# Attention results stored once a batch in whole rows, and registers of the final branch read ahead of the last product

## The chip, the cores and the metric

The kernel runs on one core of a Trainium2 chip. TensorE (PE) multiplies, VectorE (DVE), ScalarE (ACT) and GpSimd (POOL) work element by element, SyncE (SP) issues transfers, and 16 DMA engines move data between the on-chip memory and DRAM. Each engine has its own instruction stream; semaphores order them. The metric is the time of one execution on the device, in microseconds (us); lower is better.

## The reference

Two blocks one after the other. First an attention that is linear in the sequence (8 batches, 8 heads, 576 tokens, 64 channels a head): softmax of q over the channels, softmax of k over the tokens, then two small products. Its result, with the heads side by side, is x, 576 rows of 512 numbers for each batch. Then a mixture of depths: of each batch's 576 tokens, the 128 with the highest score pass through a two-layer network, and what it gives is added to their rows; all other rows of the output are x itself.

```python
kv = einsum('bhsd,bhse->bhde', softmax(k, tokens), v)
x = einsum('bhsd,bhde->bhse', softmax(q, channels), kv)   # then heads side by side
scores = einsum('bsd,d->bs', x, w_gate)
out = x.copy()
for b in range(B):
    top = argpartition(-scores[b], 128)[:128]
    ye = maximum(x[b, top] @ w1, 0) @ w2                  # 512 -> 1024 -> 512
    out[b, top] = x[b, top] + sigmoid(scores[b, top])[:, None] * ye
```

## The kernel before, in words

**Units.** The attention is cut into 16 units; a unit is one batch and half of its heads (`units`, line 96; `NQ` is 2). Unit 2b is the first half of the heads of the kernel's batch b, unit 2b+1 the second half. `place(b)` (line 93) gives the batch in memory, (b - 1) mod 8, so the kernel's first batch is the last in memory.

**One unit.** `load` fetches k, v and q; `k_exp`, `q_exp` (ACT) take exponentials; `v_copy` lays v beside a column of ones; `kv_mm` forms the product of k and v on PE and `kv_out` scales it on DVE; `q_t` or `q_blocks` turns q; `x_mm` forms the result on PE; `x_sums` takes the score sums; `x_scale` (line 436) divides by the softmax sum and writes the tile `xs[b]`. That tile holds both units of a batch. A partition holds nine tokens in all, split into two groups: partitions 0 to 63 hold the first five token rows of each run of nine, partitions 64 to 127 the other four. So `x_store(u)` (line 449) issues two DMAs a unit from SP: 64 partitions times 5 rows, and 64 partitions times 4 rows, each row 1 KB, half a row of the output.

**One batch.** After both of its units, `score`, `score_row` and `compare` rank the tokens; `hits` marks the chosen ones; `find` (line 514) makes the list of row numbers with a small product on PE; `fetch` (line 530) reads those rows back from the output in DRAM with an indirect DMA of POOL, so it must wait until the stores of that batch have landed. The row range that it names begins at row 0, so it waits for the indirect writes of the batches below it too. `turn` (line 566) transposes the rows on PE, `mlp1` (line 582) and `mlp2` (line 597) are the two layers, `finish` (line 635) adds the result to the rows on DVE, and `put` (line 604) writes them to the output with an indirect DMA. The first batch takes another way (`select`), without reading back.

**Order.** The order of all instructions is written out by hand. Stage s works on unit s of the attention while it loads unit s+3 and runs the network of the batch before. `queues(s, last)` (line 842) sets what SP issues in stage s, from the string `QUEUE` (line 824): `x+0 kv+3 q+3` is the store of unit s, then k and v of unit s+3, then q of unit s+3. In stage 5 the stores of units 0 and 1 (`x-5 x-4`) follow at the end. Stage 3 issues the stores of units 2 and 3 itself. SP takes its queue strictly in order. Some loads wait for a product of the stage (`last`) and for the fourth load before them (`way`).

**The end.** `last_product` (line 619) computes the second layer of the last batch in two halves, 16 products each, and writes each half by an indirect DMA. After it, `nc.values_load` (line 989) reads the number `number` (made by `count_good`, line 738) into a register of every engine. `tc.If` (line 990) then enters `general()`, a slower way for inputs out of range, when not all checks held; with these inputs it is passed by.

Of the kernel before, what the change touches and what calls it, by code (L numbers as in the profile page):

```python
# [17 lines left out]
def kernel(  # L18
# [23 lines left out]
    nc = tc.nc  # L42
    B, H, S, D = q.shape
    DM, F = moe_w1.shape
    P = 128
    R = 5
    N2 = R - 1
    T = R + N2
# [5 lines left out]
    NQ = H // 4  # L54
# [33 lines left out]
    def part(i):  # L88
        return slice(64 * i, 64 * i + 64)
# [3 lines left out]
    def place(b):  # L93
        return (b - 1) % B
# [77 lines left out]
    def clear(u):  # L172
        for what in "kv":
# [5 lines left out]
                                               ap=[[DM, 1], [1, DM]]))  # L179
# [239 lines left out]
    xs = {}  # L419
# [28 lines left out]

    def x_store(u):
        b, qd = units[u]  # L450
        for n, rows in enumerate((R, N2)):
            nc.sync.dma_start(
                out=bass.AP(tensor=out.tensor, offset=out[place(b), n * R].offset + 4 * D * qd,
                            ap=[[T * DM, 64], [DM, rows], [1, 4 * D]]),
                in_=xs[b][part(n), :rows, qd].rearrange("p r i a d -> p r (i a d)"))


    def score(b, up=2):
# [200 lines left out]
    def each(step, b, *args):  # L659
        for n in range(n_sl):  # L660
            step(b, n, *args)
# [26 lines left out]
    def general():  # L688
# [4 lines left out]
        for b in range(B):  # L693
            for u in (NQ * b, NQ * b + 1):
                load(u, "kvq", flat=True)
                shift(u)
                k_exp(u)
                q_exp(u, 0)
                q_exp(u, 1)
                v_copy(u)  # L700
                kv_mm(u)
                kv_out(u)
                q_t(u, 0)
                q_t(u, 1)
                for i in range(2):
                    x_mm(u, i)
                    x_out(u, i)
                x_store(u)
            score(b, 0)
            score_row(b, 1.0)  # L710
            for r in range(R):
                compare_exact(b, r)
            for step in (hits, find, fetch, gate):
                each(step, b)
            each(turn, b)
            for f in range(KF):
                each(mlp1, b, f)
            for f in range(KF):
                each(mlp2, b, f)
            each(finish, b)  # L720
            each(put_done, b)

    CHECKS = 6

    def in_range():

        rq, rk = qrec.rearrange("p u a i n -> p (u a i n)"), krec.rearrange("p u n -> p (u n)")
        sc = s_all.rearrange("p b r -> p (b r)")
        ends = md.tile([P, CHECKS], F32, tag="ends", name="ends", bufs=1)
        good = md.tile([P, CHECKS], BF16, tag="good", name="good", bufs=1)  # L730
        for n, (src, op, bound) in enumerate(((rq, OP.max, 1.0 / LOW), (rk, OP.max, 1.0 / LOW), (sc, OP.max, FAR),
                                              (rq, OP.min, LOW), (rk, OP.min, LOW), (sc, OP.min, -FAR))):
            nc.vector.tensor_reduce(out=ends[:, n:n + 1], in_=src, axis=AX.X, op=op)
            nc.vector.tensor_scalar(good[:, n:n + 1], ends[:, n:n + 1], bound, None,
                                    op0=OP.is_le if op == OP.max else OP.is_ge)
        return good

    def count_good(good):
        g_ps = pair("kv")[:, 0]
        nc.tensor.matmul(out=g_ps[:1, :CHECKS], lhsT=ones_b[:, :1], rhs=good, start=True, stop=True)  # L740
        total = md.tile([1, 1], F32, tag="total", name="total", bufs=1)
        nc.vector.reduce_sum(out=total, in_=g_ps[:1, :CHECKS], axis=AX.X)
        number = md.tile([1, 1], I32, tag="number", name="number", bufs=1)
        nc.vector.tensor_copy(out=number, in_=total)
        return number
# [79 lines left out]
    number = good = None  # L825
    for s in range(LAG, NU + LAG - 1):
# [15 lines left out]
        def queues(s, last):  # L842
            for what in QUEUE.get(s, QUEUE["odd" if s % 2 else "even"]).split():
                name, u = what[:-2], s + int(what[-2:])
                if name == "x":
                    if u < NU:
                        x_store(u)
                elif u < NU:
                    load(u, name, after=last, odd=False if name == "q" and u in SPREAD else None)
                    last = None  # L850
# [14 lines left out]
        if s == LAG:  # L865
# [7 lines left out]
            x_out(2, 0)  # L873
            x_out(2, 1)
            x_store(2)
            load(5, "q")
            pieces(2)
# [32 lines left out]
        else:  # L910
# [59 lines left out]
            if good is not None and number is None:  # L970
                pieces(0, to=6)
                number = count_good(good)
# [11 lines left out]
        if s == NU:  # L984
            good = in_range()

    each(last_product, B - 1)

    ok = nc.values_load(number[0:1, 0:1], min_val=0, max_val=CHECKS * P)
    with tc.If(ok != CHECKS * P):  # L990
        general()

# [23 lines left out]
```

## Time and profile before

| | us |
|---|---|
| median of three runs | 206.79 |
| lowest, highest run | 206.05, 208.31 |
| the profiled execution, its own time | 204.39 |
| span of that execution, first to last instruction | 202.6 |
| PE busy, DVE busy, ACT busy, POOL busy | 190.1, 127.2, 91.7, 39.3 |
| DMA issues of the store (line 452) | 32, median 0.636 each on SP |

The profile is one execution with the hardware profiler on. Times in it count from the start of the span. "Busy" is the time that an engine's own instructions took; reading registers, waiting and issuing transfers are not in it. The 40 slices cut the span into equal parts, each digit a busy share in tenths. The chain is followed back from the last instruction: at each step to what released it. A row `SPq L452 <- DVE xs L439: 13.4, 5, 3.9` says that SP's queue waited at line 452 for the DVE instruction of line 439, for 13.4 us in total, 5 times, at most 3.9.

### The profile page before, as it was taken

The page shows a single profiled execution, that of the slowest core. Times are in us where ns is not written, and L with a number is a line of the kernel's source. Part 1 is how long each engine was busy: PE and PEld are TensorE (multiplying, and loading weights), DVE is VectorE, ACT ScalarE, POOL GpSimd, SP SyncE. Part 2 cuts the span into 40 slices and gives each one's busy share as a digit, 9 for nine tenths or more (in the row PEclk, how much of TensorE's full clock was granted, in tenths as well). Part 3 has the DMA queues.
Part 4 walks back from the last instruction along what each step waited for, and adds up shares of the span by engine and source line. Part 5 has one row for each costly group of instructions (what it writes and reads, how often), then busy time and mean ns, then how long its engine had stood idle before and what let it go on. Part 6 is the DMA issues. An engine that isn't in the chain of part 4 may idle for free.

```text
span 202.6 us, 6720 instructions
## 1 busy us (share of the span) xinstructions
PE 190.1 (94%) x2817; PEld 146.7 (72%) x2817; DVE 127.2 (63%) x395; ACT 91.7 (45%) x136; POOL 39.3 (19%) x107
## 2 busy tenths in 40 slices
PE   7889899989999999999999999999999999999950
PEld 3567789986599657977598749964895789469840
DVE  5778935889278364866678477838697879232000
ACT  3477776590946555629046543654363021111100
POOL 7302100101020400412040402210040122313130
PEclk9999999999999999999999999999999999999997
DMA  6999999999888999999899899999996156211110
GB/s 212 394 293 315 379 368 373 363 383 374 246 263 241 300 348 330 260 283 308 191 280 275 293 236 269 255 323 201 269 279 231 55 120 151 68 54 55 57 40 23
DMA packets 35255, 49.43 MB, mean 244 GB/s; under 512 B 2449, under 2 KB 28049, under 8 KB 35218
## 3 DMA queue, kind: packets, MB, share of 16 engines
q1 hardware_dynamic: 33296, 42.72, 69.5%
q0 software_dynamic: 1776, 5.92, 9.5%
q8 instruction: 24, 0.39, 0.8%
q10 hardware_dynamic: 146, 0.30, 0.5%
q14 instruction: 13, 0.11, 0.2%
HBM read 37.39 MB, written 11.53 MB: 241 GB/s over the span
## 4 chain that ended last, share of the span: by engine, by line
PE 75%; DMA 15%; SPq 4%; ACT 1%; issue 1%; POOL 0%; POOLq 0%; DVE 0%; ACTq 0%
PE mm L591 26%; PE mm L601 24%; DMA k<-in_k_dram 15%; PE kv L336 8%; PE x L414 6%; PE mm L628 3%; PE x L384 2%; PE mm L571 2%; PE kv L479 2%; SPq L152 2%; SPq L187 1%; PE x L405 1%; ACT ke L289 1%; PE mm L520 1%; SPq L146 1%
## 5 line engine op out<-in xcount | busy, mean ns | idle before, releaser
L591 PE MATMUL mm<-xT,w 128*128 128x128 f32 x512 | 61.8, 278 | 0.5 <-DVE xT L579 0.3
L591 PEld LDWEIGHTS mm<-xT,w 128*128 128x128 f32 x512 | 58.7, 192 | 2.3 <-ACT xT L579 1.0
L601 PE MATMUL mm<-w,hT 128*128 128x512 f32 x112 | 52.5, 603 | 0.0
L493 DVE SCALAR_TENSOR_TENSOR junk<-srow,s,not_before 128x576 bf16<-128x576 f32 x40 | 32.7, 818 | 4.4 <-ACT srow L485 3.3
L601 PEld LDWEIGHTS mm<-w,hT 128*128 128x128 f32 x112 | 19.7, 190 | 17.7 <-issue 17.2
L289 ACT ACTIVATE ke<-k 128x1280 f32<-128x1280 f32 (+1 forms) x16 | 20.2, 1261 | 10.2 <-DMA k<-in_k_dram 10.2
L439 DVE TENSOR_TENSOR xs<-x,qrec 128x640 f32<-128x640 f32 (+1 forms) x31 | 23.4, 756 | 0.6 <-issue 0.3
L336 PEld LDWEIGHTS kv<-v_ones,ke 128*64 128x64 f32 x560 | 17.5, 137 | 4.5 <-issue 3.2
L336 PE MATMUL kv<-v_ones,ke 128*64 128x65 f32 x560 | 19.4, 224 | 0.5 <-ACT srow L485 0.5
L414 PE MATMUL x<-kv_w,qT 64*64 64x66 f32 x960 | 19.4, 221 | 0.1
L307 ACT COPY v_ones<-v 128x1280 f32<-128x1280 f32 x14 | 17.6, 1254 | 3.4 <-DMA v<-in_v_dram 3.4
L594 ACT ACTIVATE hT<-mm 128x512 f32<-128x512 f32 x16 | 9.5, 596 | 20.5 <-PE mm L591 20.5
L414 PEld LDWEIGHTS x<-kv_w,qT 64*64 64x64 f32 x960 | 17.1, 134 | 1.8 <-issue 1.2
L463 POOL TENSOR_TENSOR s<-s_all,valid_r 128x5 f32<-128x5 f32 x8 | 1.5, 192 | 85.0 <-DVE s_all L461 85.0
L534 POOL DMA_INDIRECT xr<-out_dram,idx x8 | 8.1, 1012 | 48.8 <-DVE no L526 31.6
L579 ACT COPY xT<-mm 128x512 f32<-128x512 f32 x7 | 4.1, 585 | 27.3 <-PE mm L571 27.3
L391 ACT COPY qT<-x 128x640 f32<-128x640 f32 (+1 forms) x18 | 10.8, 648 | 12.3 <-PE x L384 11.6
L302 ACT ACTIVATE qe<-q 128x640 f32<-128x640 f32 (+1 forms) x22 | 13.9, 677 | 3.5 <-DMA q<-in_q_dram 3.5
L345 DVE RECIPROCAL krec<-kv 128x2 f32<-128x2 f32 x16 | 2.7, 169 | 18.0 <-PE kv L336 17.3
L639 DVE SCALAR_TENSOR_TENSOR o<-mm,g,xr 128x512 f32<-128x512 f32 x6 | 4.5, 751 | 11.4 <-PE mm L601 11.4
L485 ACT ACTIVATE srow<-kv 128x576 f32<-128x576 f32 x7 | 4.5, 648 | 12.3 <-PE kv L479 12.3
L431 DVE RECIPROCAL qrec<-x 128x10 f32<-128x10 f32 (+1 forms) x31 | 6.6, 213 | 4.8 <-PE x L405 4.3
(125 smaller groups left out, 204.2 us busy)
## 6 DMA issues: line engine op xcount, KB each, us to landing
out_dram<-xs SPq DMA_DIRECT2D x16, 320.0 KB, 4.5
k<-in_k_dram SPq DMA_DIRECT2D x14, 320.0 KB, 4.9
v<-in_v_dram SPq DMA_DIRECT2D x14, 320.0 KB, 6.5
w<-in_moe_w_dram SPq DMA_DIRECT2D x8, 512.0 KB, 7.6
out_dram<-xs SPq DMA_DIRECT2D x16, 256.0 KB, 5.5
q<-in_q_dram SPq DMA_DIRECT2D x7, 576.0 KB, 6.7
q<-in_q_dram SPq DMA_DIRECT2D x14, 280.0 KB, 7.0
k<-in_k_dram SPq DMA_DIRECT2D x14, 256.0 KB, 6.6
```

Of the source, the lines that this page charges most:

```text
L289: nc.scalar.activation(out=ke, in_=view(raw["k"][u % LD], u not in FLAT), func=AF.Exp)
L302: nc.scalar.activation(out=st["qe", u][:, r0:r1], in_=qr[:, r0:r1], func=AF.Exp)
L307: engine.copy(out=out_v, in_=in_v)
L336: nc.tensor.matmul(out=kv_ps[part(i), a, :D + 1], lhsT=ke[:, 2 * i + a, r], rhs=vo[:, 2 * i + a, r], start=(r == 0), stop=(r == N2))
L391: nc.scalar.copy(out=to, in_=src)
L414: last = nc.tensor.matmul(out=to, lhsT=rows, rhs=kw[part(i), a], start=True, stop=True)
L439: nc.vector.tensor_mul(xs[b][:, :n, qd, :, a].rearrange("p r i d -> p i r d"), x[:, :, :, :D], qrec[:, u, a, :, :n].to_broadcast([P, 2, n, ...
L493: nc.vector.scalar_tensor_tensor(junk, st["srow", b], st["s", b][:, r:r + 1], not_before[:, r], op0=OP.subtract, op1=OP.is_ge, accum_out=s ...
L534: nc.gpsimd.indirect_dma_start(out=xr[:m], out_offset=None, in_=out_rows[:(place(b) + 1) * S], in_offset=bass.IndirectOffsetOnAxis(ap=st[" ...
L591: st["piece"] = nc.tensor.matmul(out=h_ps[:, f % 4 * m:(f % 4 + 1) * m], lhsT=w1[:, d, f * P:(f + 1) * P], rhs=xT[:, d, :m], start=(d == 0 ...
L594: nc.scalar.activation(out=hT[:, f - 3:f + 1, :m], in_=h_ps[:, :4 * m].rearrange("p (f c) -> p f c", f=4), func=AF.Relu)
L601: st["piece"] = nc.tensor.matmul(out=st["y", b, n][:m], lhsT=st["hT", b, n][:, f, :m], rhs=w2[:, f], start=(f == 0), stop=(f == KF - 1))
```

## The change

Two edits. The store of a batch's first unit is left out. The store of its second unit writes the whole rows of both: 64 partitions, each five rows of 2 KB that lie one after the other in memory and in the tile, 10 KB in one run; and 64 partitions of four rows, 8 KB. The number of bytes is the same. In stage 3, the store of unit 2 falls away and that of unit 3 carries both; in stage 5, `x-5` falls away and `x-4` carries units 0 and 1.

The second edit moves the reading of the registers from behind `last_product` to in front of it.

```diff
     def x_store(u):
         b, qd = units[u]
+        if qd < NQ - 1:
+            return
         for n, rows in enumerate((R, N2)):
             nc.sync.dma_start(
-                out=bass.AP(tensor=out.tensor, offset=out[place(b), n * R].offset + 4 * D * qd,
-                            ap=[[T * DM, 64], [DM, rows], [1, 4 * D]]),
-                in_=xs[b][part(n), :rows, qd].rearrange("p r i a d -> p r (i a d)"))
+                out=bass.AP(tensor=out.tensor, offset=out[place(b), n * R].offset, ap=[[T * DM, 64], [1, rows * DM]]),
+                in_=xs[b][part(n), :rows].rearrange("p r q i a d -> p (r q i a d)"))
...
+    ok = nc.values_load(number[0:1, 0:1], min_val=0, max_val=CHECKS * P)
     each(last_product, B - 1)
 
-    ok = nc.values_load(number[0:1, 0:1], min_val=0, max_val=CHECKS * P)
     with tc.If(ok != CHECKS * P):
         general()
```

## The prediction

> **What bounds the kernel.** I read the page first (busy shares, slices, the chain), then busy time by stretch, then the stores and whoever waits for them, then the end.
>
> ```profile
> span 202.6 us, 6720 instructions
> PE 190.1 (94%) x2817; PEld 146.7 (72%) x2817; DVE 127.2 (63%) x395; ACT 91.7 (45%) x136; POOL 39.3 (19%) x107
> DMA  6999999999888999999899899999996156211110
> PE 75%; DMA 15%; SPq 4%; ACT 1%; issue 1%; POOL 0%; POOLq 0%; DVE 0%; ACTq 0%
> ```
>
> TensorE and the DMA engines are both nearly full, and the chain says who decides when: its 15% of DMA all lies before 40 us (loads of k), where no store has been issued. From there it runs over TensorE. The stretches 42 to 180, 180 to 195.2 and 195.2 to the end confirm it (time, then busy time and count of PE, PEld, DVE, ACT, POOL; clock; DMA share; GB/s):
>
> ```profile
> 42.00:180.00 138.00, 138.00 (x2059) 103.67 (x2054) 94.21 (x279) 62.91 (x93) 24.97 (x61) 1.00 0.86 249
> 180.00:195.20 15.20, 15.03 (x98) 13.30 (x97) 3.62 (x16) 1.71 (x3) 4.21 (x4) 1.00 0.14 47
> ```
>
> TensorE has no hole in 138 us, at full clock. Nothing that only lightens the DMA engines or SP there can gain; a transfer that lands too late can lose. The question is which data TensorE takes with little to spare.
>
> **Stores, part by part.** The source view of the store, and the longest of SP's own waits after 42 us (total, times, longest):
>
> ```profile
> L452 SPq DMA_DIRECT2D out_dram<-xs x32: 595/636/1767, 37.2 to 168.2; - x32
> SPq L452 <- DVE g L562: 34.6, 6, 11.1
> ```
>
> Removed: 16 of 32 issues, 16 x 0.64 = 10 us of SP; each remaining one carries twice the bytes (640 and 512 KB for 320 and 256). In even stages the loads of unit s+3 stood behind a store that waited for the scaling; they now go straight to the queue: at stage 12, SP's store begins at 140.1 and the load of k at 141.5, and the former falls away. I cost this at nothing: the cover is TensorE's unbroken work. Without that cover it would be worth some microseconds of earlier loads. The order of SP's queue is otherwise kept, no wait is added there, and in odd stages k(s+3) stands behind 1152 KB instead of 576. While the queue is backed up, that is the same number of bytes ahead of it as before, since the other 576 KB were ahead already, one stage earlier. The tightest load is k of unit 6, behind store 3: its exponential starts at 50.52 after 4.82 us of waiting for DMA, the copy of v after it ends at 54.18, TensorE wants both at 55.23: 1.05 us to spare. The DMA engines are at 383 GB/s from 44 to 48, so I take 0 for it. At stages 7, 9 and 11 the even loads before them pay the debt: in stage 8 the last product ends at 93.85, yet the store starts at 96.58 and k only at 98.01, up to 4 us that the load gains, against the 1.9 + 0.95 us that half a batch's stores take (below).
>
> What has no later load to hide behind is the last batch. Its rows are read back by an indirect DMA, which must wait for the stores of unit 15 and for the put of batch 6. DMA issues at 167 to 168.1 (the first row is unit 15's store, the second the put; size, us to landing):
>
> ```profile
> out_dram<-xs SPq DMA_DIRECT2D x1, 320.0 KB, 3.6
> out_dram<-o,idx POOLq DMA_INDIRECT x1, 5.4
> ```
>
> The timeline (start, duration), and the source view of the transposes that take the rows:
>
> ```profile
> 168.07 1.06 POOL L606 DMA_INDIRECT out_dram<-o,idx  x1 [0.55 <-issue]
> ...
> 174.52 0.97 POOL L534 DMA_INDIRECT xr<-out_dram,idx  x1 [5.39 <-DVE no L526]
> ...
> 178.53 0.14 PEld L571 LDWEIGHTS mm<-ident,xr 128*128 128x128 f32 x1 [0.24 <-issue]
> L571 PEldq EVENT_SEMAPHORE  x2: 51/51/51, 162.0 to 177.9; - x2
> ```
>
> The put lands at 168.07 + 5.4, about 173.45; the read starts at 174.52, when DVE has made the row numbers. A DMA landing frees POOL about 0.8 us later (batch 6: its last store lands at 150.82 + 6.1 = 156.9, its read starts at 157.75), so the put could be 174.52 - 0.8 - 173.45 = 0.3 us later at no cost. TensorE's sequencer passes its wait for the read at 177.9; the first weight load is at 178.53: 0.6 more. So about 0.9 us of delay is free, and the rest falls one for one on TensorE, with the whole last product behind it. Behind the waiting transposes lie two products, the first layer of batch 7 and the last product.
>
> How late will it be? Windows of store 14 alone, first half, then second half; then store 15; then idle:
>
> ```profile
> 163.50:165.25 1.75, 1.75 (x78) 1.61 (x77) 1.21 (x5) 0.58 (x1) 0.00 (x0) 1.00 0.94 178
> 165.25:166.25 1.00, 1.00 (x11) 0.95 (x10) 0.93 (x4) 0.00 (x0) 0.34 (x3) 1.00 0.94 276
> 168.75:170.50 1.75, 1.75 (x18) 1.75 (x17) 1.68 (x5) 0.60 (x1) 0.38 (x1) 1.00 0.95 175
> 173.00:174.50 1.50, 1.50 (x9) 0.62 (x8) 0.38 (x3) 0.60 (x2) 0.00 (x0) 1.00 0.00 0
> ```
>
> Before, store 15 takes 327,680 B / 175 + 262,144 B / 276 = 1.9 + 0.95 = 2.8 us from 168.75, so to 171.6; the put's rest ends 1.4 us later, at 173.0. After, the sum has two ends. Slow: the same pace per half, 655,360 / 178 + 524,288 / 276 = 3.7 + 1.9 = 5.6 us, 2.8 more. Fast: the pace of 44 to 48 us, 1,179,648 / 383 = 3.1 us, 0.3 more.
>
> Here the **Trainium skill** says two opposite things. "DMA: Bandwidth & Descriptors", section "Rules for kernel authors", wants small transfers joined into large ones: rows of 10 and 8 KB instead of 1 KB pieces, the fast end. "SBUF — State Buffer", section "Door 1: The DMA port swizzle", has 64 partitions such as 0 to 63 reach 8 of 16 ports, half of about 436 GB/s[...]: an estimate of 1,179,648 / 218 = 5.4 us. The trace agrees with that for the first half (178 and 175) but not for the second (276, above 218). I take the middle of the slow and fast ends, 4.3 us, 1.5 more than before. Then the put lands at 174.95, the read starts at 175.75, 1.2 late; less the 0.6, TensorE stalls **0.6 us**. Fast end: 0. Slow end: 173.45 + 2.8 + 0.8 - 174.52 - 0.6 = 1.9 us. Below nothing it can't go: the index, not the store, starts the read today.
>
> **Registers.** Views of the read's line and of the end of the chain:
>
> ```profile
> L989 PEldq TENSOR_LOAD <-number x1: 487/487/487, 191.2 to 191.2; - x1
> L989 POOLq TENSOR_LOAD <-number x1: 514/514/514, 195.7 to 195.7; - x1
> 195.75 0.51 POOLq L989
> 196.26 0.68 POOL out_dram L631
> ```
>
> The chain puts POOL's 0.51 us in front of the last indirect store, which would be a gain of 0.51. But that store's own record starts at 195.98, 0.28 after the DVE result, and the first half's at 192.53, also 0.28 after its own (192.25): the read runs beside it. After it everything waits for the landing at about 198.9. So 0 gain, bound 0.5. Cost: five engines now read before the last product. SP reads at 186.7 as before; ACT has nothing behind it (its last relu precedes the read); on DVE, two results; on POOL, two indirect stores; on PE, the 32 matmuls of L628 queue behind the wait for `number`, which DVE finishes at 186.65. PE's read ends near 187.2 and L628's first weight load was at 188.00, under 16 matmuls still running from 186.2 to 188.3. Cover 0.8 us; if it is gone, 0.5 us. Before, PE's sequencer made its read at 191.2, 4 us ahead of its matmuls, so it does run ahead. I take 0.
>
> **Sum.** The profiled execution took 204.39 us (span 202.6 and 1.8 around it). 204.39 + 0.6 = 205.0. The median of the runs is 206.79, 2.4 above the profiled execution; I add the difference to the median: **207.4 us**.
>
> **Rivals.** (a) Nothing visible at the tail: bytes packed in 10 KB rows land within the free 0.9 us, and POOL's read does leave the path: 204.39 + 0 - 0.5 = 203.9, on the median 206.3. For: chain and the full pace at 44 us. Against: the 0.28 us twice. (b) Slower: the port pace of a half holds for large rows too. Price: 1.9 at the tail, and at unit 6 the two rows of store 3 take 5.6 instead of 3.1 us, so k lands 2.5 later, less 1.05 to spare: 1.45. Together 3.4, so 210.2. It costs something once the doubled store needs more than 2.8 + 0.9 = 3.7 us, and over 1% (2.07 us) near 5.0, where the two stalls are 1.3 and 0.8. For: 175 and 178 in both isolated stores. Against: at 44 us stores were in the mix and it ran at 383. (c) Earlier loads feed TensorE sooner and gain over 1%: only before 41.5 us does TensorE wait for loads, and those were issued before the first store. (d) The rows are still cut into 1 KB pieces: the isolated last store then keeps the slow pace, 1.9, and the backed-up one at 44 us its own: 208.7.
>
> **Numbers.** Forecast (0.2 to 1.3 us slower) 0.5; (a) 0.2; (b) and (d) 0.25; (c) and other gains 0.05. The runs of before spread 206.05 to 208.31, so within 1% is about all a measurement of this kernel can tell from no change. The range goes from a little below (a), 205.8, to most of (b), 209.8. Slower by over 1% (above 208.86) is (b), (d) and a tip of the forecast.
>
> **What would show it.** Right: 16 stores, the indirect read of the last batch 1 to 1.5 us later, a hole of some 0.6 us in TensorE before L571, k of unit 6 no later than 50.5. Registers: PE's read near 187 and no gap before L628. Wrong: a gap in TensorE between 42 and 175 us, an indirect read of an earlier batch that TensorE waits for, or the last store leaving POOL much sooner than 0.28 us after DVE.

## The result, and the profile after

The changed kernel is slower: 213.59 us (212.28 to 214.34), beside 206.42 us (204.48 to 208.31) for the kernel before, a ratio of 1.037 (95% interval 1.027 to 1.047). Ratios and intervals, here and below, leave out executions that lie more than 1.5% above the fastest of their kernel, while medians are of all executions. The prediction was 207.4, with a range from 205.8 to 209.8. The profiled execution of after took 214.34 us, with a span of 212.5. That is 9.9 more than the span of before, where the medians differ by 7.2: the profile of before is of an execution faster than all of the four (204.39), that of after of the slowest of its four.

The page of after: span, busy time, busy share of the DMA engines in 40 slices, and the chain that ended last.

```profile
span 212.5 us, 6689 instructions
PE 192.2 (90%) x2815; PEld 147.5 (69%) x2817; DVE 127.0 (60%) x395; ACT 92.1 (43%) x136; POOL 38.7 (18%) x107
DMA  6999999999919899999959999999999206531110
PE 47%; DMA 26%; DVE 13%; issue 6%; POOL 3%; ACT 1%; POOLq 0%; DVEq 0%; ACTq 0%
```

The chain has left TensorE: its share fell from 75% to 47%. DMA rose from 15% to 26%, and now lies on the path from 50 us on. The DMA row has two new holes, a 1 at slice 12 and a 5 at slice 21, where before had 8 and 9. Busy time by stretch shows them (columns as in the prediction), first after:

```profile
42.00:189.50 147.50, 139.55 (x2053) 104.17 (x2050) 93.91 (x279) 63.00 (x92) 25.21 (x61) 1.00 0.84 231
58.00:64.00 6.00, 5.83 (x112) 5.59 (x113) 3.51 (x10) 3.14 (x5) 1.32 (x7) 1.00 0.27 88
106.00:112.00 6.00, 6.00 (x116) 5.93 (x116) 4.84 (x15) 3.90 (x6) 2.44 (x8) 1.00 0.62 141
```

and the same two short stretches of before:

```profile
58.00:64.00 6.00, 6.00 (x79) 5.93 (x71) 5.06 (x14) 4.00 (x6) 1.31 (x7) 1.00 0.91 275
106.00:112.00 6.00, 6.00 (x47) 4.66 (x45) 4.75 (x12) 3.61 (x4) 0.68 (x1) 1.00 1.00 278
```

TensorE now has 8 us of holes between 42 and 189.5, at full clock, where it had none. In two stretches the DMA engines stand idle for (0.91 - 0.27) x 6 = 3.8 and (1.00 - 0.62) x 6 = 2.3 us more than before. Everything they don't move there, they must move later.

What they move later is seen in the chain of after. Its long DMA pieces (start, duration) are these; `o,idx` is a put, `xr` the rows read back:

```profile
50.33 7.80 DMA xr<-out_dram,idx
...
110.53 9.87 DMA out_dram<-o,idx
121.20 6.67 DMA xr<-out_dram,idx
133.05 9.47 DMA out_dram<-o,idx
143.32 8.29 DMA xr<-out_dram,idx
...
177.21 7.84 DMA out_dram<-o,idx
```

So the put of an earlier batch takes 9 to 10 us (7.8 at the end), the read-back begins 0.8 us after it has landed, and TensorE waits. In the trace two things wait for that landing: POOL's queue ahead of the read, and VectorE, which then writes the row numbers (line 526) that the read needs. The read of batch 5 is the clearest. DMA issues of before in that stretch, put and read:

```profile
out_dram<-o,idx POOLq DMA_INDIRECT x1, 6.6
xr<-out_dram,idx POOLq DMA_INDIRECT x1, 8.1
```

and the timelines of TensorE, before and then after:

```profile
143.64 0.66 PE L571 MATMUL mm<-ident,xr 128*128 128x128 f32 x4
```

```profile
148.69 1.39 PE L336 MATMUL kv<-v_ones,ke 128*64 128x65 f32 x40 [0.43 <-ACT v_ones L307]
151.65 0.66 PE L572 MATMUL mm<-ident,xr 128*128 128x128 f32 x4 [1.57 <-DMA xr<-out_dram,idx]
```

The read takes the same time, 8.3 for 8.1; the put in front of it takes 2.9 us more. Its packets show where: in after it is issued at 133.05, but its rows move from 138.62 to 142.17, the first 1.3 us after the last packet of the first half of the doubled store (137.36). In before it is issued at 127.18, and its rows move from 130.57 to 133.35. Before, the read had 1.0 us to spare (it landed at 142.62). That margin exists at each batch, and the DMA records and the weight loads of the transposes give it:

| batch | 1 | 2 | 3 | 4 | 5 | 6 | 7 |
|---|---|---|---|---|---|---|---|
| before: us from landing of the rows to their first use | 2.5 | 3.0 | 2.0 | 2.1 | 1.0 | 0.6 | 0.7 |
| after | 0.04 | 0.2 | 2.9 | 0.04 | 0.04 | 1.4 | 0.1 |

After, the rows of five of seven batches are used within 0.22 us of landing.

Matching each weight load of TensorE in after with the same one in before gives where the delay grows, 10.3 us in all up to the transposes of batch 7:

| | us |
|---|---|
| waits for read-back rows: batches 1, 4, 5, 7 | 1.57 + 0.12 + 1.64 + 1.21 = 4.5 |
| waits for k or v, at 55.28 and 148.69 | 0.10 + 0.50 = 0.6 |
| holes with no wait, in runs of matmuls | 2.05 + 0.83 + 0.69 + 0.68 + 0.39 + 0.30 + 0.25 = 5.2 |
| ahead of 42 us | -0.05 |

The third row is the surprise. In the timeline of TensorE in after, the largest of these holes:

```profile
84.52 0.60 PE L480 MATMUL kv<-ident,s_all 128*128 128x128 f32 x4
86.95 0.27 PE L480 MATMUL kv<-ident,s_all 128*128 128x128 f32 x1 [1.83 <-issue]
```

Four of five equal matmuls run, the fifth comes 1.83 us later, and no semaphore stands between them. The same work runs unbroken in before.

### The profile page after: what moved, and what is told of

Same layout as the page of the kernel before. It is cut to its first block, busy times and chain, and to the rows that moved or that the text cites. A ratio compares the mean times of both kernels' runs of the same rounds, so it can differ in the third digit from the quotient of the medians.

```text
span 212.5 us, 6689 instructions
## 1 busy us (share of the span) xinstructions
PE 192.2 (90%) x2815; PEld 147.5 (69%) x2817; DVE 127.0 (60%) x395; ACT 92.1 (43%) x136; POOL 38.7 (18%) x107
## 2 busy tenths in 40 slices
DMA packets 26806, 49.42 MB, mean 233 GB/s; under 512 B 2193, under 2 KB 18577, under 8 KB 25746
## 4 chain that ended last, share of the span: by engine, by line
PE 47%; DMA 26%; DVE 13%; issue 6%; POOL 3%; ACT 1%; POOLq 0%; DVEq 0%; ACTq 0%
PE mm L592 16%; DMA out_dram<-o,idx 13%; DMA xr<-out_dram,idx 12%; PE mm L602 10%; PE x L414 6%; PE kv L336 4%; DVE junk L494 3%; PE mm L572 2%; PE mm L552 2%; PE mm L629 2%; PE x L384 1%; DVE xs L439 1%; DVE qrec L431 1%; PE kv L480 1%; DMA out_dram<-o,idx_h 1%
## 5 line engine op out<-in xcount | busy, mean ns | idle before, releaser
L414 PE MATMUL x<-kv_w,qT 64*64 64x66 f32 x960 | 21.0, 222 | 1.6 <-issue 1.3
L414 PEld LDWEIGHTS x<-kv_w,qT 64*64 64x64 f32 x960 | 17.9, 133 | 4.0 <-issue 3.2
L345 DVE RECIPROCAL krec<-kv 128x2 f32<-128x2 f32 x16 | 2.7, 169 | 14.5 <-PE kv L336 13.7
```

The costliest lines, as they stand in the source:

```text
L414: last = nc.tensor.matmul(out=to, lhsT=rows, rhs=kw[part(i), a], start=True, stop=True)
```

## Experiments

The theories were these. **Pieces**: the large pieces (10,240 and 8,192 bytes) are bad for whatever shares the DMA engines with them. **Burst**: 1152 KB leave at once, in front of the loads, put and read-back, where before half had left a stage earlier. **Half**: one half of the partitions that is written alone is slow, and the whole rows make that stretch longer. **Registers**: the second edit costs.

**Registers alone.** The stores are those of before; only the reading of the registers is moved.

> The registers read ahead of the last product, the stores as before. My working: no change, 206.4 plus or minus 0.5 us. If POOL's read had been on the path of the last indirect store: about 0.5 us faster, 205.9 or less; in the trace the end of the span comes 6.2 us after the last indirect store starts, as in the changed kernel, where it was 6.6 us before. If the wait for the number holds TensorE's queue: a hole of 0.3 to 0.5 us ahead of the last product, and that much slower.

Measured: 206.02 us, ratio 1.002 (0.996 to 1.008). The second edit has no effect that the times can show (the trace shows a small one, below). So the loss is the store's.

**Larger pieces, same time.** The store stays once a unit, but its pieces are 5 and 4 KB. For that the tile is laid out by halves, and so is the output: its half rows stand in another order than the reference's, and a row that is read back holds parts of two tokens. The bytes and the DMAs are the same in number.

```diff
-            xs[b] = xp.tile([P, R, NQ, 2, 2, D], F32, tag="xs", name="xs", bufs=3)
+            xs[b] = xp.tile([P, NQ, R, 2, 2, D], F32, tag="xs", name="xs", bufs=3)
...
-                            ap=[[T * DM, 64], [DM, rows], [1, 4 * D]]),
-                in_=xs[b][part(n), :rows, qd].rearrange("p r i a d -> p r (i a d)"))
+                            ap=[[T * DM, 64], [1, rows * 4 * D]]),
+                in_=xs[b][part(n), qd, :rows].rearrange("p r i a d -> p (r i a d)"))
```

> One store a unit as before, but in pieces of 5 and 4 KB: the tile holds a unit's rows together and they go to memory in one run, so the two halves of each group of rows stand in another order in the output; nothing is left out. Piece theory: slower than before by about half of the change's loss or more, 209 to 213 us, with holes of TensorE inside rows of matmuls. Burst theory: as before, 205 to 208 us.

Measured: 205.12 us, ratio 0.998 (0.994 to 1.003). A piece five times as large changes nothing that can be measured, while the stores leave once a unit.

**Late, in 1 KB pieces.** All four DMAs of a batch are issued in the second unit's place of SP's queue, those of the first unit first.

```diff
+        if qd < NQ - 1:
+            return
+        for qd in range(NQ):
             for n, rows in enumerate((R, N2)):
```

> Both units of a batch are stored in the second unit's stage, as in the change, but with the store's old 1 KB pieces (four DMAs a batch), and the registers read where they were before. Burst theory (twice the bytes at once in front of the loads and the read-back is what costs): as slow as the changed kernel, 212 to 214 us, with the waits of TensorE for the rows read back in batches 1, 5 and 7. Piece theory (a DMA engine that holds 8 to 10 KB pieces lets everything else queue behind them: loads, indirect DMAs, TensorE's instructions): within 1% of before, 205 to 208, no hole inside a row of matmuls.

Measured: 207.43 us, ratio 1.006 (0.999 to 1.013). The trace shows that this was not quite the experiment that I had meant. SP had issued its loads and came to the store early, and the first unit's DMAs left as soon as their half was ready: unit 14's at 165.12, unit 15's at 170.79. So the even stages' loads do go ahead of the store here, and the bytes still leave in two portions in five of the eight batches (2 to 5 and 7; in 6 all four are issued between 153.4 and 156.1); that costs 0.6% (1.3% at most).

**The burst in 1 KB pieces.** The same, with the second unit's DMAs ahead of the first unit's, so that both must wait for the second.

```diff
+        for qd in reversed(range(NQ)):
             for n, rows in enumerate((R, N2)):
```

> In the trace of the last such run each unit's 1 KB stores still left as soon as that unit's half of the tile was ready, because SP was through with its loads by then. Here the second unit's DMAs stand first in the queue, so both units' stores leave together once the second unit is scaled: the change's moment with the old 1 KB pieces, 320 and 256 KB a DMA. Burst theory (what costs is that all 1152 KB go in one go, in front of the loads of the odd stage, the put and the read-back): 211 to 215 us, like the changed kernel. Half-run theory (what costs is 640 KB in a row from partitions 0 to 63, at about 185 GB/s): here the halves alternate at 320 and 256 KB as before, so 205 to 208 us.

Measured: 212.86 us, ratio 1.037 (1.027 to 1.046). The pieces are those of before, and the loss is that of the change. Between this run and the last only the order of the units differs, and with it the moment at which half of the bytes leave.

**Whole rows in 2 KB pieces.** Four DMAs a batch, first the two of partitions 0 to 63, then the two of 64 to 127.

```diff
+            for r0 in range(2):
+                nc.sync.dma_start(
+                    out=bass.AP(tensor=out.tensor, offset=out[place(b), n * R + r0].offset,
+                                ap=[[T * DM, 64], [2 * DM, (rows + 1 - r0) // 2], [1, DM]]),
+                    in_=xs[b][part(n), r0:rows:2].rearrange("p r q i a d -> p r (q i a d)"))
```

> Whole rows once a batch in the second unit's stage, in pieces of 2 KB (even and odd rows in DMAs of their own, four a batch), registers read where they were. Piece theory: near before, 205 to 208.5 us. Burst theory: as the changed kernel, 212 to 214 us.

Measured: 214.26 us, ratio 1.034 (1.027 to 1.041). Its DMA issues (put and read-back, number, median us to landing):

```profile
xr<-out_dram,idx POOLq DMA_INDIRECT x8, 8.7
out_dram<-o,idx POOLq DMA_INDIRECT x6, 6.2
```

(The eighth read is that of the first batch's rows, which are needed once at the end.) With pieces of 2 KB the put takes 6.2 us, as before (6.1), not 8.7 as in after. But now the read-back takes 8.7, where before has 4.9 and after 6.2. Together they take 14.9 here as in after, and 13.1 in the burst of 1 KB pieces (6.0 and 7.1), against 11.0 in before. Which of the two is late is not settled by the size of the pieces: the kernel without the tail, below, has the large pieces and takes 6.8 and 6.1.

**Who pays: loads ahead of the store.** The change's stores, but in the odd stages k, v and q are issued ahead of the store.

```diff
-    QUEUE = {"odd": "x+0 kv+3 q+3", "even": "x+0 kv+3 q+3", 5: "x+0 kv+3 q+3 x-5 x-4"}
+    QUEUE = {"odd": "kv+3 q+3 x+0", "even": "x+0 kv+3 q+3", 5: "kv+3 q+3 x+0 x-5 x-4"}
...
-            x_store(3)
             load(6, "kv")
             load(6, "q")
+            x_store(3)
```

> As the change stores, but in the odd stages the loads of k, v and q stand ahead of the store in SP's queue, not behind it. If the loads behind the doubled store are what delays TensorE (the waits of the exponential of k rose from 6.6 to 13.7 us in all), this wins most of the loss back: ratio 1.00 to 1.015. If it is the rows that are written and read back behind the burst (put, indirect read), they get later still: the transposes of batches 1, 5 and 7 start later than in the changed kernel, ratio 1.04 or more.

Measured: 226.86 us, ratio 1.094 (1.088 to 1.100). The timeline of TensorE in this kernel, transposes of batch 5, and two stretches around them:

```profile
162.88 1.12 PE L572 MATMUL mm<-ident,xr 128*128 128x128 f32 x4 [10.06 <-DMA xr<-out_dram,idx]
```

```profile
152.80:162.80 10.00, 0.03 (x2) 0.00 (x0) 1.04 (x4) 0.00 (x0) 1.02 (x1) 0.63 0.96 231
162.80:172.00 9.20, 9.12 (x116) 8.66 (x117) 4.67 (x13) 3.64 (x6) 2.38 (x8) 0.66 0.28 58
```

The waits for k do shrink, to 3.9 us in all from 13.7 in after. But TensorE stands still for 10 us at batch 5, 3.0 at batch 1, until the read-back rows come. What can least be late is the line of store, put, read-back and transposes, more than the loads.

**The tail alone, and all but the tail.** First only batch 7 is stored whole, then only batches 0 to 6.

```diff
+        whole = b == B - 1        # the second kernel: b < B - 1
+        if whole and qd < NQ - 1:
+            return
```

> Only the last batch is stored once, in whole rows; the other seven are stored once a unit as before, and the registers are read where they were before. This is the tail alone. The burst theory says: in the changed kernel the transposes of batch 7 started 1.63 - 0.37 = 1.26 us late on top of all earlier delay, so the same here, no other new hole in TensorE, ratio about 1.006 (1.000 to 1.010). The prediction's own size for this step was 0.6 us, ratio 1.003; its slow end 1.9 us, 1.009. The rival that the earlier delays of the changed kernel made its end worse says about 1.000.

> Batches 0 to 6 are stored once, in whole rows; the last one once a unit as before; registers as before. If the effects of the batches add up, this costs what the change costs (7.2 us) less the 1.3 us of the tail: ratio about 1.029 (1.02 to 1.037), with the late reads at batches 1 and 5 and the holes without a wait in it, and no hole of more than 0.3 us in front of the transposes of batch 7. If the tail is what matters, it is near 1.01.

Measured: 207.85 us, ratio 1.006 (1.002 to 1.009), and 210.75 us, ratio 1.024 (1.019 to 1.029), on one chip against the same runs of before (206.26). The tail costs 1.2 us, the other seven batches 4.9. Together that is 1.030, inside the interval of the change. Most of the loss is not in the tail, where the prediction looked for it. The second expectation held for the time and for the transposes of batch 7, which no hole precedes. Of the late reads it had only a part: batch 1 shows no wait, batches 4 and 5 wait 0.45 and 0.38 us, and most of what TensorE lost in that profile are holes without a wait (table further down).

**A bit left in its old place.** One token row in nine of partitions 0 to 63 (64 KB) still leaves once a unit; the rest leaves whole in the second unit's place.

```diff
+        nc.sync.dma_start(
+            out=bass.AP(tensor=out.tensor, offset=out[place(b), 0].offset + 4 * D * qd, ap=[[T * DM, 64], [1, 4 * D]]),
+            in_=xs[b][part(0), 0, qd].rearrange("p i a d -> p (i a d)"))
+        if qd < NQ - 1:
+            return
+        for n, r0, r1 in ((0, 1, R), (1, 0, N2)):
```

> As the change stores, but one token row in nine of the partitions 0 to 63 (64 KB of a unit's 576) still leaves once a unit, in its old place in SP's queue. So the loads of the even stages stand behind a store again, as before, while 1024 KB still leave in one go in the odd stages. If the loads that start earlier are what empties the DMA engines and so what makes the burst late, this returns most of the way to before: ratio 1.00 to 1.015, and no empty slice near 60 and 108 us. If the size of the burst itself is the cause, it stays like the change: 1.03 to 1.04.

Measured: 211.49 us, ratio 1.026 (1.021 to 1.031), between the two expectations. The DMA row of its page:

```profile
DMA  6999999999968999899999899999988216431100
```

The loads of the even stages are held back again and the two holes have nearly closed (6 and 8 in place of 1 and 5). Yet more than two thirds of the loss stays. The idle engines are at most a part of the cause; the portion that leaves in one go is the larger.

**The order of the halves.** Three runs mix the two halves of the partitions instead of writing one after the other. Two of them have whole rows: in four DMAs that take turns (6, 4, 4 and 4 KB pieces), and in two DMAs of which POOL issues the second; a third has the stores of before with POOL issuing the second half.

```diff
+        for n, r0, r1 in ((0, 0, 3), (1, 0, 2), (0, 3, 5), (1, 2, 4)):
...
+            (nc.gpsimd if n else nc.sync).dma_start(
```

> Whole rows once a batch, but cut into four DMAs that alternate between the two halves of the partitions: 6 KB pieces of the first half, 4 KB of the second, 4 and 4. Burst theory: 211 to 215 us. Half-run theory: 205 to 208 us.

> The change's stores, with the second half of the partitions issued by POOL instead of SP, so that both halves move at the same time; registers where they were. If the pace of a half is what stretches the burst: the last batch's 1152 KB take about 3.1 to 3.8 us instead of 5.3, the last read-back comes 1 to 2 us earlier, and the whole takes 208 to 211 us. If the burst's bytes alone decide: 212 to 215 us, as the changed kernel.

> The kernel before with the second half's store of each unit issued by POOL. If halves together move faster, a unit's store takes about 1.6 instead of 2.7 us where nothing else moves; since TensorE doesn't wait for stores in the kernel before, the time stays as before, 205 to 207 us. Slower by 1 us or more if POOL's queue, which now waits for the scaling, holds up a put or a read-back.

Measured: 209.56 us (207.55 to 213.12; too few runs for a ratio; before 205.41); 210.37 us, ratio 1.016 (1.007 to 1.026); 206.81 us, ratio 1.007 (1.004 to 1.011). Mixing the halves seems to win back about half of the loss, although a second queue alone costs 0.7%. But the burst in 1 KB pieces mixes the halves too, and won nothing. So the last pair keeps the pieces at 2 KB and changes only the order of the four DMAs: the two loops swapped, and beside it the kernel of 2 KB pieces again.

```diff
-        for n, rows in enumerate((R, N2)):
-            for r0 in range(2):
+        for r0 in range(2):
+            for n, rows in enumerate((R, N2)):
```

> The same four DMAs a batch as in the store in 2 KB pieces (ratio 1.0341), in another order: the two halves of the partitions take turns instead of one half after the other. If the slow pace of a half that is written alone is a part of the loss, this is faster than that kernel by what the whole rows in alternating halves won over the change (209.6 against 213.6 us, without an interval): ratio 1.015 to 1.025, and the put lands about 6 us after its issue instead of 9 to 10. If only the number of bytes that leave in one go counts, it stays at 1.03 to 1.04.

> The store in 2 KB pieces, one half after the other, beside the kernel of alternating halves on the same chip and against the same runs of before: the difference of the two is the price of the order of the halves alone. Half-pace theory: this one is 1 to 2 per cent slower than the other. Bytes alone: both the same, 1.03 to 1.04.

Measured: 210.52 us, ratio 1.017 (1.008 to 1.026), and 212.20 us, ratio 1.032 (1.024 to 1.039). The expectation of the half theory held for the times, though the two intervals overlap at their ends, and the medians of all runs differ by 0.8% only. Its other part, a put of 6 instead of 9 to 10 us, had no ground: the 2 KB kernel of one half after the other has 6.2 already. At 2 KB the order of the halves seems to be worth up to about 1.5%; why it is worth nothing at 1 KB stays open.

## Why the prediction was wrong, step by step

**What bounds the kernel.** Right for before, but for one detail: the loads on the chain end at 39.55, and the first store is issued at 37.2, not after them. That what lightens SP and the DMA engines gains nothing held too: 16 issues fewer on SP, no gain. The remark that a transfer which lands too late can lose was the important one, and it was then followed for one load of k and for the last batch only. Its own sign of being wrong, "an indirect read of an earlier batch that TensorE waits for", is what came.

**The stores of batches 0 to 6, costed at nothing. This is the step that failed.** In its words: "While the queue is backed up, that is the same number of bytes ahead of it as before, since the other 576 KB were ahead already, one stage earlier", and "At stages 7, 9 and 11 the even loads before them pay the debt". Two things are wrong in it. The queue isn't always backed up: the earlier loads ran the engines dry at 58 to 64 and at 106 to 112 us, and idle time doesn't pay a debt. And the loads were the wrong thing to ask after. The waits of the exponential of k and of the row numbers show it (after 42 us; total, times, longest), first in before, then in after:

```profile
ACT ke L289 <- DMA k<-in_k_dram: 6.6, 3, 4.8
...
DVE idx L525 <- DMA out_dram<-o,idx: 3.0, 2, 2.2
```

```profile
ACT ke L289 <- DMA k<-in_k_dram: 13.7, 5, 5.9
...
DVE idx L526 <- DMA out_dram<-o,idx: 12.1, 4, 4.1
```

k did come later, but ScalarE took up most of it and TensorE lost 0.6 us to loads. The wait for the put rose fourfold, and behind it stands the read-back of every batch, whose margins of 0.6 to 3.0 us (first table) were in the trace of before for each batch, not for the last alone. The cost of this step was 4.9 us by the run without the tail, against 0. TensorE lost it in two ways: waits for the rows, and holes without a wait, to which the prediction gave no term.

The runs show that the portion leaving in one go is the cause: 1.037 with the old pieces in one portion, 1.006 with the same loads ahead and mostly two portions, 0.998 with larger pieces and two portions. How much of it is the slow pace of a half is not settled: at 2 KB the order of the halves is about half of the loss (1.017 for 1.032), at 1 KB mixed halves lose as much as the change. The way from the burst to the loss is shown for the put, the read and the transposes, by the profile and by the run that made that line later still. That is a part of the loss only; for the holes without a wait the way is less sure (below).

**The tail, 0.6 us.** The mechanism was right, the size was off. DMA issues of after at 176.65, then timelines of POOL and TensorE:

```profile
out_dram<-xs SPq DMA_DIRECT2D x1, 640.0 KB, 5.0
```

```profile
185.82 0.97 POOL L535 DMA_INDIRECT xr<-out_dram,idx  x1 [7.55 <-DVE g L562]
...
189.27 0.63 PE L572 MATMUL mm<-ident,xr 128*128 128x128 f32 x4 [1.02 <-DMA xr<-out_dram,idx]
```

The term that was mis-sized is the time of the doubled store, 4.3 us as the middle of 3.1 and 5.6. Its packets run from 177.77 to 184.09: 6.3 us. Those of the first half end at 181.29: 655,360 B in 3.5 us are 186 GB/s, near the pace of the half before (178). Rows of 10 KB are hardly faster than pieces of 1 KB here. The second half took 3.0 us and not 1.9; the rows of the put move in the same stretch (from 182.54). They did so in before too: store 15's packets run from 168.76 to 172.44, 3.7 us, where the prediction read 2.8. The growth is thus 2.6 us, not 1.5.

The put landed after 7.84 instead of 5.36 us, 2.5 later, and the read came 0.77 after it (0.8 in the prediction). The sum's own form then gives 2.5 - 0.3 - 0.6 = 1.6, and the first weight load did come 1.58 us later against TensorE's work; 0.37 of it is regained at once, since in before the second weight load had waited until 178.96. Net 1.2 us, which is also what the run with the tail alone has (0.59%). (The put that the prediction gives to batch 6 is batch 5's, as line 945 puts `mlp_b - 1`; the sum does not depend on it.) The delay of the put is near the slow end (2.8), not at the middle: the nearest row was an isolated store of the same half, and the 383 GB/s came from a mix of loads and stores.

Of the two rules of the Trainium skill that the prediction weighed, the one on joining ("DMA: Bandwidth & Descriptors", section "Rules for kernel authors") gave nothing here: it speaks of transfers under 64 KB, and those of before had 320 and 256 KB already. The one on ports ("SBUF — State Buffer", section "Door 1: The DMA port swizzle") had the right sign, while the 186 GB/s lie below its 218 for a half.

**Registers, 0.** Right as far as the times can tell; the trace shows 0.4 us that the prediction argued away. The source view of the read in after:

```profile
L988 POOLq TENSOR_LOAD <-number x1: 512/512/512, 197.0 to 197.0; - x1
L988 PEldq TENSOR_LOAD <-number x1: 487/487/487, 197.0 to 197.0; - x1
```

PE's read ran under the matmuls of the first layer, with no hole before line 629. From the start of the last indirect store to the end of the span it is 212.5 - 206.33 = 6.2 us, beside 202.6 - 195.98 = 6.6 in before. The difference is the store's landing: 2.55 us after its start in after and 2.53 in the kernel with the registers alone, but 2.87 to 3.30 in all fourteen kernels in which POOL reads the register just ahead of it. So the read, whose 0.51 us seemed to run beside the store (its record starts 0.27 us after the result), does delay what the store writes. It is 0.2% of the time, less than the interval of the run with the registers alone.

**The rivals.** (b) was the nearest. Its pace of the half held at the tail, and its chain of reasoning (a doubled store that delays what queues behind it) is what happened; but it put the price at k of unit 6, where 0.1 us was lost and not 1.45, and saw no other place, so that it ended at 210.2. (a) and (c) fell: nothing gained. (d) fell: the packets number 26,806, not 35,255, so the rows did become long, without any use.

**Holes without a wait, in no part of the prediction.** They are half of what TensorE lost in the profiled execution. The same matching, each kernel against the profile of before, from 42 us to the transposes of batch 7:

| us that TensorE lost | for rows | for k, v | without a wait |
|---|---|---|---|
| registers alone | 0.0 | 0.2 | 1.0 |
| pieces of 5 and 4 KB, two portions | 0.0 | 0.0 | 1.1 |
| 1 KB, mostly two portions | 0.6 | 0.0 | 2.0 |
| after | 4.5 | 0.6 | 5.2 |
| burst in 1 KB pieces | 3.3 | 0.0 | 3.6 |
| whole rows but for a bit | 3.1 | 1.0 | 2.2 |
| all but the tail | 0.9 | 0.0 | 4.2 |

The waits for rows come with the burst. The holes without a wait are larger with it in these profiles, and they are most of the loss in the run that isolates the step that failed; but some 1 us of them is there without any burst, and the split differs from profile to profile: in the three profiles of 2 KB pieces the rows cost 5.3 to 8.2 us and the holes 0.2 to 3.2.

What the traces show is that instructions came late. The queue of instructions has packets of 16 KB. In after one runs from 84.24 to 85.39; the hole began at 85.1 and ended at 86.95. In before the corresponding one came at 79.04, 3.9 us ahead of the same place in the work (82.97). After 42 us the kernels have nine holes of 0.7 us or more between matmuls without a wait, in seven of them. They lie at only two places of the program (those that before reaches at 82.97 and 115.0), and each ends 1.3 to 1.6 us after the end of such a packet. Of the smaller holes some do the same; most stand beside no packet, and stay unexplained. That a burst is what makes these packets late is inferred; no experiment here tested it.

## What to carry to other kernels

A store that leaves in two portions beside other traffic may be better than one of half as many DMAs: joining it here made no byte faster, and put twice the bytes ahead of a put and a read-back. Before moving bytes in a shared queue, list for every later transfer on the way to the bounding engine how long before its use it lands, in each iteration; margins of 0.6 to 3 us were used up here by a burst that takes 6 us where it stands alone. "The same bytes were ahead of it before" holds, even for the loads, only where the engines never run dry in between.

## What the runs showed of the hardware

- One half of the partitions (0 to 63) written alone went at 175 to 186 GB/s, with pieces of 1 KB and of 10 KB alike.
- A put issued behind a store waits for it: in after its rows began to move 5.6 us after its issue (133.05 to 138.62), in before, behind half the bytes, 3.4 us (127.18 to 130.57). The moving itself took 3.6 and 2.8 us.
- SP's own issue of k behind a doubled store took 2.3 and 2.6 us (at 111.22 and 113.61), where it took 1.3 and 1.6 before.
- An indirect store of POOL whose engine reads a register just ahead of it landed 2.87 to 3.30 us after its start (14 kernels), and 2.53 and 2.55 us where the read came earlier (2 kernels).
- A long hole costs twice: after the 10 us hole in the kernel with the loads ahead, the granted clock of TensorE was 0.66 for the next 9 us (the row above), so its matmuls ran at about 0.6 of their pace (1.12 us for four transposes that else take 0.66). The holes of up to 2 us in after left the clock at 1.00. But a hole of 1.6 us (at 117.3, two queues) and one of 1.8 us (at 149.2, the second run of 2 KB pieces) were each followed, within 1.1 us of their end, by 3.4 us at a clock of 0.50. So the length of a hole alone does not tell whether it costs clock.
